# An attention and MLP block whose rounded keys and queries are stored once and repeated by the loads, with another order of work at the start and the fourth pair's load moved ahead of the third's

## The chip, the core and the metric

The kernel runs on one core of one Trainium2 chip. A core has a tensor engine (PE; PEld is its weight load), a vector engine (DVE), a scalar engine (ACT), GpSimd (POOL) and a sync engine (SP), whose queue issues nearly all transfers of this kernel, and sixteen DMA engines that carry them out. The metric is the device time of one execution in microseconds; the time of a kernel is the median of its runs. The profile is one further execution.

## The reference

One transformer block on `x` of 2048 rows by 512, in fp32, with a conditioning vector `c`:

```python
mod = (_silu(c) @ w_mod).reshape(c.shape[0], 6, 1, -1)
sa, ca, ga, sb, cb, gb = (mod[:, 0], mod[:, 1], mod[:, 2], mod[:, 3], mod[:, 4], mod[:, 5])
h = _layernorm(x, axis=-1) * (1 + ca) + sa
x = x + ga * _A_ref(h, A_wqkv, A_wo)      # 32 heads of 16, full softmax, output projection
h = _layernorm(x, axis=-1) * (1 + cb) + sb
x = x + gb * _B_ref(h, B_w1, B_b1, B_w2)  # dense to 1792, x*tanh(softplus(x)), dense to 512
```

## The kernel before

**Split operands.** The tensor engine is fed numbers in a rounded format (fp32r). To keep the accuracy, an operand is split into a rounded part (`hi`) and the rounded rest (`lo`), and a product is computed as hi*hi + hi*lo + lo*hi. For the scores the three products are folded into one contraction: a head has 16 channels, and 48 rows of a 64-row half of the array hold, for each channel, the keys' hi, lo, hi against the queries' hi, hi, lo. Two more rows of the query tile hold the negated row maxima, against ones in the key tile.

**Stages.** A start computes the conditioning columns (`modc`), the layer norm, its transposition (`h_h`, `h_l`: the hi and lo parts of the normalized rows, channels on the partitions) and the first slices of keys, queries and values, block by block of 512 rows (`tr_tb`, four blocks). Keys and queries of eight heads go to DRAM scratch (`kscr`, `qscr`) in the function `put` of `qk_unit`, and come back as pair tiles by `load_k` and `load_q`: a pair is two heads, one on partitions 0 to 47 (keys) or 0 to 49 (queries), the other on 64 to 111 or 64 to 113. The keys of a pair are 48 rows of 8 KB per head, the queries 50 rows of 2 KB. Five pairs fit (`NR`, tiles `ka`, `qa`).

**The main loop.** 512 steps t, sixteen to an iteration n of two pairs (2n and 2n+1), 32 iterations: 8 groups of four heads for each of four blocks of queries. A step has eight score products (L588, exponentials on ACT, L591), eight products for the row maxima of a later iteration, 20 steps ahead (L539 with its reduction on DVE, L541; in the 20 steps before t = 0 they are taken two at a time, L553), a few products of the projections or the MLP (L139), and the product with the values (L606). The maxima of an iteration's first pair begin at t = 16n - 20, those of its second at t = 16n - 12.

**What sets the order.** The schedule is written out by hand. `at(h, f)` runs `f` at half step h (two to a step): the position in each engine's program, not a time. The queue of SP takes its entries in order, and an entry that must wait for a buffer or for data holds all behind it. Pair 2n+1 is put in the queue at half step 32(n - 1), pair 2n at 32(n - 2) plus 2, 9 or 15; before t = 0, pairs 0 and 1 are loaded block by block within the start, and pairs 2 and 3 at the half steps of a small table (`for pp, h in ((2, -22), (3, -8))`). Row sums (`sm`), reciprocals (`rc`, `rscr`), broadcasts (`rb`, from a DRAM row read sixteen times) and the negated maxima (`mt`) take the same queue, and so do weights (`w`, `hl`, `ep`, `wm`, `wr`), values (`vq`, `vscr`, `vg`).

**PSUM.** Products go through a ring of six banks. `free_banks` takes out dependencies between instructions that only share the ring's tensor, if they touch other banks and no common tile.

Of the kernel before, what the change touches and what calls it, by code (L numbers as in the profile page):

```python
# [8 lines left out]
F32 = mybir.dt.float32  # L9
# [9 lines left out]
def adaln_block(ctx: ExitStack, tc: tile.TileContext, x, wqkv, wo, w1, b1, w2, c, w_mod, out):  # L19
# [21 lines left out]
    LOV = ((1,), (), (1, 3), (1, 3))  # L41
# [10 lines left out]
    nc.scalar.preload_act_table_set("natural_log_exp_and_others")  # L52
# [4 lines left out]
    kscr = dram.tile([H, 48, S], F32, name="kscr")  # L57
    qscr = dram.tile([H, 50, S], F32, name="qscr")
# [16 lines left out]
    sel = cst.tile([P, 1], F32, name="sel")  # L75
    nc.gpsimd.memset(sel, 0.0)
    for k in range(DK):
        nc.gpsimd.memset(sel[32 * k:32 * k + 1, :], 1.0)
# [89 lines left out]
    def free_banks():  # L168


        seen = []
        for i in nc.cur_bb.bb.instructions:
            banks, names, made = set(), set(), set()
            for a in (*i.outs, *i.ins):
                v = getattr(a, "bass_ap", None)
                if v is not None and v.tensor.name != ring_t.tensor.name:
                    names.add(v.tensor.name)
                    if any(a is w for w in i.outs):
                        made.add(v.tensor.name)
# [66 lines left out]
    def qk_unit(kind, ct, tb, tag):  # L246
# [7 lines left out]
        def fin(h=None):  # L254
            qh = qp.tile([P, TB], F32R, tag="qh", name="qh", bufs=2)
            ql = qp.tile([P, TB], F32R, tag="ql", name="ql", bufs=2)
            if h is None:
                hi_copy("a", qh, acc)
                lo_sub("v", ql, acc, qh)
            else:  # L260
                qf = pw.tile([P, TB], F32, tag="raw", name="qf", bufs=1)
                nc.scalar.copy(qf, acc)  # L262
                hi_copy("p", qh, qf)
                lo_sub("p", ql, qf, qh)
            scr, rows = (qscr, 50) if kind == 0 else (kscr, 48)
# [12 lines left out]

            put() if h is None else at(clear(h + (5 if h > 60 else 2)), put)
# [26 lines left out]
    def load_q(pp, rows=50):  # L306
# [5 lines left out]
        for s in range(2):  # L312
            nc.sync.dma_start(qt[64 * s:64 * s + rows, :], qscr[h + s, :rows, qb * TB:(qb + 1) * TB])

    def load_k(pp, tb=None):
# [3 lines left out]
        at_ = slice(0, S) if tb is None else slice(tb * TB, (tb + 1) * TB)  # L319
        assert {(1, h // 8, i) for i in (range(NB) if tb is None else (tb,))} <= put_away, (pp, put_away)  # L320
        for s in range(2):
            nc.sync.dma_start(kt[64 * s:64 * s + 48, at_], kscr[h + s, :, at_])
# [6 lines left out]
    with ExitStack() as es:  # L329
        lp = es.enter_context(tc.tile_pool(name="lp", bufs=1))  # L330
        cc = lp.tile([P, DK], F32, name="cc")
        nc.sync.dma_start(cc, c.rearrange("o (k p) -> p (o k)", p=P))
# [7 lines left out]
        wma = [lp.tile([P, DK, D], F32, name=f"wma{i}") for i in range(2)]  # L340
# [13 lines left out]
        nc.gpsimd.memset(zer, 0.0)  # L354
        for i in range(NR):
            nc.gpsimd.memset(qa[i].bitcast(F32), 0.0)
        for i in range(2):
            nc.gpsimd.memset(ka[i].bitcast(F32), 1.0)

        e = lp.tile([P, DK], F32, name="sil_e")  # L360
# [3 lines left out]
        nc.vector.tensor_mul(sil, cc, e)  # L364

# [21 lines left out]
        def first_norm():  # L387

            mv = lp.tile([P, 4, 2], F32, tag="ln_mv4", name="ln_mv4", bufs=2)
            rs = lp.tile([P, 4, 4], F32, tag="ln_rs4", name="ln_rs4", bufs=3)  # L390
            for h in range(2):
                two = slice(2 * h, 2 * h + 2)
                for i in range(2 * h, 2 * h + 2):
                    st_ = lp.tile([P, 6], F32, tag="ln_st", name="ln_st", bufs=4)
                    nc.vector.bn_stats(out=st_, in_=xts[i])
                    nc.vector.bn_aggr(out=mv[:, i, :], in_=st_)
                nc.gpsimd.tensor_scalar(rs[:, 0, two], mv[:, two, 1], 1.0, EPS, op0=ALU.mult, op1=ALU.add)
                nc.gpsimd.tensor_scalar(rs[:, 3, two], mv[:, two, 0], -1.0, 0.0, op0=ALU.mult, op1=ALU.add)
                nc.gpsimd.tensor_tensor(rs[:, 1, two], rs[:, 0, two], nhalf.to_broadcast([P, 2]), op=ALU.pow)
                nc.gpsimd.tensor_mul(rs[:, 2, two], rs[:, 3, two], rs[:, 1, two])  # L400
                if h == 0:
                    hi_k = split_hi(1, 0)
            return rs, hi_k

        def split_hi(kind, i, eng="p"):
# [4 lines left out]
        def split_lo(kind, i, hi):  # L410
            lo = lp.tile([P, DK, P], F32R, tag="wl", name="wl", bufs=2)
            lo_sub("p", lo, slices[kind, i], hi)
            slices[kind, i] = (hi, lo)

        def first_apply(rs, i, eng):
            xt = xts[i]
            if eng == "a":
                nc.scalar.activation(xt, xt, AF.Identity, scale=rs[:, 1, i:i + 1], bias=rs[:, 2, i:i + 1])
            else:
                nc.vector.tensor_scalar(xt, xt, rs[:, 1, i:i + 1], rs[:, 2, i:i + 1], op0=ALU.mult, op1=ALU.add)  # L420

        def first_tr():
            pts = [bank(("ring", "ms", "ring", "acc")[k]) for k in range(DK)]
            for ii in ((0,), (1,), (2, 3)):
                for k in range(DK):
                    for i in ii:
                        nc.tensor.transpose(pts[k][:, i * P:(i + 1) * P], xts[i][:, k * P:(k + 1) * P], ident)
            return pts

        def tr_tb(tb, ks=range(DK), pts=None):  # L430
            for k in ks:
# [12 lines left out]
        rs, hi_k = first_norm()  # L444
        pr, pm = [], bank()[:, :2 * DK].rearrange("p (i k) -> p i k", k=DK)
        for i in range(2):
            pr.append(ring())
            for k in range(DK):
                nc.tensor.matmul(pr[i][32 * k:32 * k + 32, :], sil[:, k:k + 1].to_broadcast([P, 32]), wma[i][:, k, :],
                                 start=True, stop=True)  # L450
        for i in range(2):
            row = lp.tile([P, D], F32, tag="hf", name="row", bufs=6)
            nc.scalar.copy(row, pr[i])
            for k in range(DK):
                nc.tensor.matmul(pm[:, i, k:k + 1], row[:, k * P:(k + 1) * P], sel, start=True, stop=True)
        for i in range(2):
            first_apply(rs, i, "a")
        split_lo(1, 0, hi_k)
        hi_q = split_hi(0, 0, "a")
        split_lo(0, 0, hi_q)  # L460
        first_apply(rs, 2, "a")
        first_apply(rs, 3, "v")
        nc.vector.tensor_scalar_add(modc[:, 1, :], pm[:, 1, :], 1.0)
        nc.vector.tensor_copy(modc[:, 0, :], pm[:, 0, :])
        stats_tb(1)
        tr_tb(0, pts=first_tr())
        apply_tb(1)
        def constants():
            for q4 in range(S // TB):
                nc.sync.dma_start(dap(qscr, 48 * S + q4 * TB, [[50 * S, H], [S, 2], [1, TB]]), zer[:64, :])  # L470
# [8 lines left out]
        for tb in range(NB):  # L479
            if tb + 2 < NB:  # L480
                stats_tb(tb + 2)
            if tb == 0:
                slice_split(2, 0, eng="v")
# [1024 lines left out]
    for pp, h in ((2, -22), (3, -8)):  # L1508
# [41 lines left out]
```

## Time and profile before

| | us |
|---|---|
| median of 3 runs (lowest, highest) | 1691.56 (1690.99, 1694.38) |
| profiled execution | 1691.02 |
| its span | 1689.2 |
| tensor engine busy | 1667.3 |
| vector, scalar, GpSimd busy | 1441.5, 1355.1, 821.1 |
| first write of `h_h` | 19.07 |
| first product of the maxima (L553) | 50.34 |
| first score of the main loop (L588) | 101.88 |

A busy time counts an instruction from its start to its modelled end, waits inside it included; the chain that ended last says which engine's work the end waited for. In a row of the timeline stand the start, the time, the engine, the line, the operation, output<-input, and a count where rows were merged; in a row of waits the waiting engine and line, what it waited for, and the total, the number and the longest of the waits. In the DMA view, each digit is the busy share of the sixteen engines in one fortieth of the window. A completion is written by a packet of 4 bytes, one from each DMA engine that took part in a transfer.

### The profile page before, as it was taken

Reading aid. Unit: us, or ns where it says so; the run is one execution under the profiler, and the core shown is the slowest. Engines: PE = TensorE matmul, PEld = TensorE weight load, DVE = VectorE, ACT = ScalarE, POOL = GpSimd, SP = SyncE. Lnnn points to the kernel's source line nnn. Section 1 sums busy time; section 2 is a strip of 40 time slices with the busy share of each in tenths; the row PEclk is TensorE's granted clock in tenths of the full one; section 3 lists DMA queues with packets and bytes.
Section 4 is the critical chain, followed back from the end, with each engine's and each line's share of the span. In section 5 each row is a group of like instructions: output and inputs, shape, how many; then the busy total and the mean of one; then the engine's idle time right before and its main releaser. Section 6 shows DMA issues by size and latency. Waiting matters only on the chain.

```text
span 1689.2 us, 33772 instructions
## 1 busy us (share of the span) xinstructions
PE 1667.3 (99%) x12418; PEld 921.5 (55%) x12418; DVE 1441.5 (85%) x2369; ACT 1355.1 (80%) x2612; POOL 821.1 (49%) x843
## 2 busy tenths in 40 slices
PE   7999999999999999999999999999999999999999
PEld 5755655555444455555555455555555455555687
DVE  8898888888989988888889888888889888883377
ACT  6257777777778998888888998888888998889674
POOL 7555224655313564556323564556323565555442
PEclk9999999999999999999999999999999999999999
DMA  7877556777755443434355434534354533533261
GB/s 248 269 244 199 147 150 185 218 223 216 231 142 146 110 94 98 117 88 129 84 137 152 115 77 93 139 77 127 87 144 122 130 94 77 144 107 132 75 230 63
DMA packets 115406, 238.98 MB, mean 141 GB/s; under 512 B 24928, under 2 KB 50544, under 8 KB 109288
## 3 DMA queue, kind: packets, MB, share of 16 engines
q1 hardware_dynamic: 115240, 236.82, 49.9%
q8 instruction: 98, 1.61, 0.4%
q14 instruction: 68, 0.56, 0.1%
HBM read 180.48 MB, written 51.45 MB: 137 GB/s over the span
## 4 chain that ended last, share of the span: by engine, by line
PE 91%; DVE 3%; ACT 3%; DMA 2%; POOL 1%; issue 1%; SPq 0%; ACTq 0%; DVEq 0%; POOLq 0%
PE bk L606 29%; PE ring L588 22%; PE ring L539 20%; PE bk L139 11%; PE bk L132 3%; PE ring L1219 2%; PE ring L132 2%; DVE mx L541 2%; ACT pr L591 1%; PE ring L553 0%; DMA qa<-mt 0%; DMA xt<-in_A_x 0%; PE ring L922 0%; DMA kscr<-qh 0%; PE ring L568 0%
## 5 line engine op out<-in xcount | busy, mean ns | idle before, releaser
L541 DVE TENSOR_REDUCE mx<-ring 128x1 f32<-128x512 f32 x1968 | 1223.1, 682 | 150.0 <-PE ring L539 136.4
L591 ACT ACTIVATE pr<-ring 128x512 f32<-128x512 f32 x2048 | 1078.4, 603 | 207.1 <-PE bk L139 124.7
L539 PE MATMUL ring<-ka,qa 64*128 64x512 f32 x1968 | 817.9, 429 | 1.4 <-ACT pr L591 1.1
L588 PE MATMUL ring<-qa,ka 64*128 64x512 f32 x2048 | 759.1, 402 | 3.4 <-ACT pr L591 1.9
L606 PE MATMUL bk<-pr,vg 128*32 128x512 f32 x4096 | 545.1, 604 | 0.0
L539 PEld LDWEIGHTS ring<-ka,qa 64*128 64x128 f32 x1968 | 350.5, 184 | 326.2 <-DVE mx L541 251.3
L588 PEld LDWEIGHTS ring<-qa,ka 64*128 64x128 f32 x2048 | 373.7, 184 | 194.7 <-DVE mx L541 111.4
L139 PE MATMUL bk<-h,w 64*128 64x512 f32 (+1 forms) x1080 | 278.1, 390 | 0.0
L139 PE MATMUL bk<-w,a_h 64*128 64x512 f32 x632 | 210.9, 413 | 0.0
L139 PEld LDWEIGHTS bk<-h,w 64*128 64x128 f32 x1080 | 178.5, 184 | 9.3 <-ACT pr L591 1.5
L606 PEld LDWEIGHTS bk<-pr,vg 128*32 128x32 f32 x4096 | 81.2, 108 | 135.4 <-issue 126.0
L139 PE MATMUL bk<-w,a_l 64*128 64x512 f32 x316 | 124.0, 392 | 0.0
L139 PEld LDWEIGHTS bk<-w,a_h 64*128 64x128 f32 x632 | 106.8, 184 | 4.3 <-ACT hb L800 1.0
L978 POOL TENSOR_TENSOR y<-yd,y 128x512 f32<-128x512 f32 x44 | 56.9, 1293 | 89.0 <-ACT yd L977 79.7
L812 POOL TENSOR_SCALAR qq<-ee 128x512 f32<-128x512 f32 x25 | 15.5, 619 | 169.6 <-ACT ee L806 169.6
L828 POOL TENSOR_TENSOR qq<-qq,rr 128x512 f32<-128x512 f32 x42 | 54.1, 1289 | 85.9 <-ACT rr L822 85.9
L814 POOL TENSOR_TENSOR hb<-hb,ee 128x512 f32<-128x512 f32 x42 | 54.1, 1288 | 79.6 <-DVE ee L810 77.7
L139 PE MATMUL bk<-w,o_hl 64*128 64x512 f32 x288 | 79.1, 405 | 0.0
L101 POOL TENSOR_TENSOR a_l<-hb,a_h 128x512 fp32r<-128x512 f32 x53 | 73.1, 1379 | 4.4
L98 POOL TENSOR_SCALAR qh<-qf 128x512 fp32r<-128x512 f32 x27 | 16.7, 619 | 90.8 <-ACT qf L262 69.4
L139 PEld LDWEIGHTS bk<-w,a_l 64*128 64x128 f32 x316 | 58.3, 185 | 3.4
L139 PE MATMUL bk<-h_h,wl 64*128 64x512 f32 x168 | 57.2, 420 | 0.2 <-ACT pr L591 0.2
(219 smaller groups left out, 1909.1 us busy)
## 6 DMA issues: line engine op xcount, KB each, us to landing
ka<-kscr SPq DMA_DIRECT2D x124, 384.0 KB
w<-w2scr SPq DMA_DIRECT2D x56, 512.0 KB
w<-w1scr SPq DMA_DIRECT2D x46, 512.0 KB
vg<-vscr SPq DMA_DIRECT2D x32, 552.0 KB
qa<-qscr SPq DMA_DIRECT2D x124, 100.0 KB
kscr<-qh SPq DMA_DIRECT2D x16, 512.0 KB
qscr<-qh SPq DMA_DIRECT2D x32, 256.0 KB
w2scr<-hl SPq DMA_DIRECT2D x14, 512.0 KB
```

What stands on the lines that cost most here:

```text
L101: (nc.gpsimd if eng == "p" else nc.vector).tensor_sub(lo, src, hi.bitcast(F32))
L132: nc.tensor.matmul(acc, l, r, start=start, stop=stop)
L139: i = nc.tensor.matmul(acc, l[64 * g:64 * g + 64], r[64 * g:64 * g + 64], start=start and not then, stop=bool(stop and then))
L539: nc.tensor.matmul(pm, qt[64 * s:64 * s + 64, qs * P:(qs + 1) * P], kt[64 * s:64 * s + 64, kb * TB:(kb + 1) * TB], start=True, stop=True)
L541: nc.vector.tensor_reduce(out=mxs[n][:, s, 4 * j + qs, kb:kb + 1], in_=pm, op=ALU.max, axis=AX.X)
L588: nc.tensor.matmul(p_, kt[64 * s:64 * s + 64, kc * P:(kc + 1) * P], qt[64 * s:64 * s + 64, :], start=True, stop=True)
L591: e = nc.scalar.activation(pr, p_, AF.Exp, scale=SCALE)
L606: nc.tensor.matmul(accs[n][32 * h:32 * h + 32, :], vgs[n][:, o:o + 32], pts.pop((t, h)), start=(kc == 0), stop=(kc == 15))
L814: (nc.vector if tail else nc.gpsimd).tensor_mul(hb, hb, ee)
L828: nc.gpsimd.tensor_mul(qq, qq, rr)
L978: nc.gpsimd.tensor_add(y[i], yd, y[i])
L1219: nc.tensor.matmul(po[i // 2][:, i % 2, :], l[:, s], w[:, r, :], start=(f == 0 and j == 0), stop=(f == FT - 1 and j == 2))
```

## The change

**Scratch and loads.** `kscr` shrinks from 48 to 32 rows a head and `qscr` from 50 to 34: hi once, then lo (then two rows of zeros for the queries). `put` stores hi and lo once each, for keys and queries alike, as 8 heads x 16 rows x 512. `load_q` and `load_k` now take two transfers a head in place of one: one reads the 16 hi rows twice, by a leading dimension of count 2 and step 0, into 32 partitions, the other reads the lo rows (with the two zero rows, 18 for the queries) once. A pair takes eight transfers in place of four; the rows in the tile stand in blocks of 16 (keys lo, hi, hi; queries hi, hi, lo) in place of interleaved by channel.

**Order before t = 0.** Pair 3's load moves from half step -8 to -32, ahead of pair 2's at -22.

**Start.** The x tiles are loaded first; `w_mod`'s two slices come as four tiles each; `c` is loaded as four rows by ACT's queue and transposed on PE. PE runs 38 transpositions of the identity whose result nothing reads (`keep_busy`). The conditioning sums contract on PE (`mod_sums`, accumulated over four tiles, then one transposition). The layer norm's statistics go in twos. The vector engine's `hf` is now scale times input minus `h_h` in one pass, and the shift is added by DVE or POOL. The ones in the first two key tiles are written by ACT, two query tiles' zeros move later on POOL. In `free_banks`, parts of `h_h` count as tiles of their own.

```diff
-    kscr = dram.tile([H, 48, S], F32, name="kscr")
-    qscr = dram.tile([H, 50, S], F32, name="qscr")
+    kscr = dram.tile([H, 32, S], F32, name="kscr")
+    qscr = dram.tile([H, 34, S], F32, name="qscr")
...
-                if kind == 0:
-                    for r, src in enumerate((qh, qh, ql)):
-                        nc.sync.dma_start(dap(scr, o + r * S, [[rows * S, 8], [3 * S, DH], [1, TB]]), src.bitcast(F32))
-                    return
-                hi = qh.bitcast(F32)
-                twice = bass.AP(tensor=hi.tensor, offset=hi.offset, ap=[list(hi.ap)[0], [0, 2], [1, TB]])
-                nc.sync.dma_start(dap(scr, o, [[3 * S, P], [2 * S, 2], [1, TB]]), twice)
-                nc.sync.dma_start(dap(scr, o + S, [[3 * S, P], [1, TB]]), ql.bitcast(F32))
+                for r, src in enumerate((qh, ql)):
+                    nc.sync.dma_start(dap(scr, o + r * DH * S, [[rows * S, 8], [S, DH], [1, TB]]), src.bitcast(F32))
...
-            nc.sync.dma_start(qt[64 * s:64 * s + rows, :], qscr[h + s, :rows, qb * TB:(qb + 1) * TB])
+            b, o = 64 * s, (h + s) * 34 * S + qb * TB
+            nc.sync.dma_start(qt[b:b + 32, :], dap(qscr, o, [[0, 2], [S, DH], [1, TB]]))
+            nc.sync.dma_start(qt[b + 32:b + rows, :], dap(qscr, o + DH * S, [[S, rows - 32], [1, TB]]))
...
-            nc.sync.dma_start(kt[64 * s:64 * s + 48, at_], kscr[h + s, :, at_])
+            b, o = 64 * s, (h + s) * 32 * S + at_.start
+            nc.sync.dma_start(kt[b:b + DH, at_], dap(kscr, o + DH * S, [[S, DH], [1, w]]))
+            nc.sync.dma_start(kt[b + DH:b + 48, at_], dap(kscr, o, [[0, 2], [S, DH], [1, w]]))
...
-        for i in range(2):
-            nc.sync.dma_start(wma[i], w_mod[:, i * D:(i + 1) * D].rearrange("(k p) m -> p k m", p=P))
...
         for t in range(4):
             load_x(t)
+        load_mod(0)
         slice_load(1, 0, lp, lp)
+        load_mod(1)
         slice_load(0, 0, lp, lp)
...
+        keep_busy(8)
+        cc = ring()[:, :DK]
+        nc.tensor.transpose(cc, crow, ident[:DK, :DK])
+        keep_busy(26)
...
-                nc.vector.tensor_scalar(hf, pt, modc[:, 1, k:k + 1], modc[:, 0, k:k + 1], op0=ALU.mult, op1=ALU.add)
-                lo_sub("v" if k in LOV[tb] else "p", h_l[:, k, s], hf, h_h[:, k, s])
+                nc.vector.scalar_tensor_tensor(hf, pt, modc[:, 1, k:k + 1], h_h[:, k, s].bitcast(F32), op0=ALU.mult,
+                                               op1=ALU.subtract)
+                if k in LOV[tb]:
+                    nc.vector.tensor_scalar_add(h_l[:, k, s], hf, modc[:, 0, k:k + 1])
+                else:
+                    nc.gpsimd.tensor_add(h_l[:, k, s], hf, modc[:, 0, k:k + 1].to_broadcast([P, TB]))
...
-    for pp, h in ((2, -22), (3, -8)):
+    for pp, h in ((2, -22), (3, -32)):
         at(h, lambda pp=pp: load_pair(pp))
```

The queue of SP at the end of the start, before (`ka_630` and `qa_109` are the third pair's tiles):

```order
L234 DMA wr<-in_A_wqkv 128x4x128
L1458 DMA ep<-in_B_w 128x4x128 x3
L298 DMA vscr<-vq 128x4x272
L1458 DMA ep<-in_B_w 128x4x128
L1466 DMA w1scr<-ep 128x512 x2
L1458 DMA ep<-in_B_w 128x4x128
L298 DMA vscr<-vq 128x4x272
L1466 DMA w1scr<-ep 128x512 x2
L1458 DMA ep<-in_B_w 128x4x128
L313 DMA qa_109<-qscr 50x512 x2
L322 DMA ka_630<-kscr 48x2048 x2
```

The same place now (`ka_720` and `qa_103` are the fourth pair's tiles; the sizes are those of the destination):

```order
L230 DMA wr<-in_A_wqkv 128x4x128
L1486 DMA ep<-in_B_w 128x4x128 x2
L304 DMA qa_103<-qscr 32x1x512
L305 DMA qa_103<-qscr 18x512
L304 DMA qa_103<-qscr 32x1x512
L305 DMA qa_103<-qscr 18x512
L315 DMA ka_720<-kscr 16x2048
L316 DMA ka_720<-kscr 32x1x2048
L315 DMA ka_720<-kscr 16x2048
L316 DMA ka_720<-kscr 32x1x2048
```

The fourth pair's load, eight transfers, now stands behind two of the six `ep` loads; the third pair's eight follow after four more `ep` loads, two `vscr` and four `w1scr` stores.

The queue of SP within the start, one block's stores of keys and the loads of the first two pairs' keys from it, before:

```order
L276 DMA kscr<-qh 128x2x512
L277 DMA kscr<-ql 128x512
L322 DMA ka_105<-kscr 48x512 x2
L322 DMA ka_106<-kscr 48x512 x2
L298 DMA vscr<-vq 128x4x272
```

And now:

```order
L267 DMA kscr<-qh 8x16x512
L267 DMA kscr<-ql 8x16x512
L315 DMA ka_98<-kscr 16x512
L316 DMA ka_98<-kscr 32x1x512
L315 DMA ka_98<-kscr 16x512
L316 DMA ka_98<-kscr 32x1x512
L315 DMA ka_99<-kscr 16x512
L316 DMA ka_99<-kscr 32x1x512
L315 DMA ka_99<-kscr 16x512
L316 DMA ka_99<-kscr 32x1x512
```

The two stores are 256 KB each (before 512 and 256 KB), and four loads have become eight; outside the start the pair loads keep their places among the other transfers.

More of the change, by code (lines that the diff above doesn't have):

```diff
@@ L264, in fin @@
                 lo_sub("p", ql, qf, qh)
-            scr, rows = (qscr, 50) if kind == 0 else (kscr, 48)
+            scr, rows = (qscr, 34) if kind == 0 else (kscr, 32)
             def put():
@@ L353, in adaln_block, with keep_busy @@
         zer = lp.tile([P, TB], F32, name="zer")
[L354 to L358, printed above, removed]
+        for t in qa[:3]:
+            nc.gpsimd.memset(t.bitcast(F32), 0.0)
+        spare = ring()
+        def keep_busy(n):
+            for _ in range(n):
+                nc.tensor.transpose(spare[:, :P], ident, ident)
+        keep_busy(8)
+        cc = ring()[:, :DK]
+        nc.tensor.transpose(cc, crow, ident[:DK, :DK])
+        keep_busy(26)
         e = lp.tile([P, DK], F32, name="sil_e")
@@ L364, in adaln_block @@
         nc.vector.tensor_mul(sil, cc, e)
+        hi_copy("a", ka[0], ones.to_broadcast([P, S]))
         rss = {}
@@ L451, in adaln_block @@
[L451 to L462, printed above, removed]
@@ new lines, in adaln_block @@
+        for q in range(2):
+            stats_two(q)
+        first_apply(3, "p")
+        for t in (*(t.bitcast(F32) for t in qa[3:]), zer):
+            nc.gpsimd.memset(t, 0.0)
+        mod_sums(0, (0, 1))
+        first_apply(0)
+        first_tr(0)
+        mod_sums(0, (2,))
+        first_apply(1)
+        first_tr(1)
+        mod_sums(0, (3,))
+        first_apply(2)
+        first_tr(2)
+        first_tr(3)
+        mod_cols(0)
+        hi_k = split_hi(1, 0, "a")
+        hi_copy("a", ka[1], ones.to_broadcast([P, S]))
```

121 lines of the change are left out of this document (64 added, 57 removed).

## The prediction

> **What bounds the kernel now.** I read the page first (busy shares, the chain that ended last), then the waits of the tensor engine, then the DMA view in short windows, then the timeline of the sync queue around one load.
>
> ```profile
> span 1689.2 us, 33772 instructions
> PE 1667.3 (99%) x12418; PEld 921.5 (55%) x12418; DVE 1441.5 (85%) x2369; ACT 1355.1 (80%) x2612; POOL 821.1 (49%) x843
> PE 91%; DVE 3%; ACT 3%; DMA 2%; POOL 1%; issue 1%; SPq 0%; ACTq 0%; DVEq 0%; POOLq 0%
> q1 hardware_dynamic: 115240, 236.82, 49.9%
> ```
>
> The tensor engine carries 91% of the chain. The DMA engines are busy half the time on average, with 2% of the chain: the loads are hidden. How narrowly is the question.
>
> ```profile
> PE ring L449 <- DVE sil L364: 9.2, 1, 9.2
> PE ring L588 <- DMA qa<-mt: 1.2, 1, 1.2
> ```
>
> In the waits of the tensor engine itself, one is for the start (9.2 us) and one, of 1.2 us, is for a transfer. So everything outside the first 20 us is won or lost in whether a load still comes in time.
>
> **How many engines a transfer uses.** Three windows of the DMA view, each with one kind of transfer in flight:
>
> ```profile
> DMA packets 69, 0.15 MB, mean 104 GB/s; under 512 B 4, under 2 KB 4, under 8 KB 68
> q1 hardware_dynamic: 68, 0.13, 24.7%
> DMA packets 365, 0.70 MB, mean 176 GB/s; under 512 B 22, under 2 KB 22, under 8 KB 365
> q1 hardware_dynamic: 365, 0.70, 49.3%
> DMA  0000990939990341929229197994909103000000
> DMA packets 144, 0.52 MB, mean 194 GB/s; under 512 B 16, under 2 KB 16, under 8 KB 144
> ```
>
> First pair (543.70 to 545.12 us): `rb<-rscr`, 64 rows of 2 KB, whose DRAM side is written as 4 x 16 with the 16 a repeat of step 0. It is 64 data packets and 4 completion packets, at a quarter of the sixteen engines: it runs on four. Second pair (33 to 37 us): three `qscr` stores in a row, DRAM side 8 x 16 x 512, at half of the sixteen for four microseconds: eight engines, and the same eight, since three transfers waiting on different eights would have filled sixteen. Third (976.3 to 979 us): one `w<-w1scr`, 128 rows, 16 completion packets: sixteen engines. So the number of engines follows the outermost count of the narrower side: 4, 8, 16. Per engine that is 104/4 = 26 GB/s and 176/8 = 22 GB/s; I take 25, and for a bad case 194 GB/s over the third window's 16 engines at 63.5% busy, 19.
>
> The change writes the repeated halves of its loads as `[[0,2],[S,16],[1,w]]`: outermost count 2, on 32 partitions. By the rows that is two engines, always the same two. No row has a bulk transfer with an outermost 2, so the bounds are 2 and 16 engines; I take 2, since `rb` is the same form with another count. The Trainium skill, "DMA: Bandwidth & Descriptors", section "Why a DMA increments its semaphore by 16 and not by 1", states it: the number is the largest up to 16 that divides both sides' slowest dimension, and on this path the lowest-numbered engines are taken; its "Rules for kernel authors" warn of a leading zero-stride broadcast of c copies, which leaves at most c. The trace agrees at 4, 8 and 16; at 2 no run here shows it yet.
>
> **The loads in the main loop.** The work of a pair of heads on engines 0 and 1 becomes: keys 2 x 256 KB on two engines, 2 x 131072 B / 25 GB/s = 10.5 us; queries 2 x 64 KB, 2.6 us; the 16-row and 18-row parts 1.0 us (8 KB and 4 KB per engine and half). Together 14.1 us, where the 968 KB over sixteen engines took some 4. Now the time there is, for pair 31:
>
> ```profile
> 751.26 0.67 SPq L313 DMA_DIRECT2D qa<-qscr  x2
> 751.98 0.78 SPq L322 DMA_DIRECT2D ka<-kscr  x2
> 751.41 1.06 PE L606 MATMUL bk<-pr,vg 128*32 128x512 f32 x8
> 754.24 1.06 PE L606 MATMUL bk<-pr,vg 128*32 128x512 f32 x8
> 757.13 1.06 PE L606 MATMUL bk<-pr,vg 128*32 128x512 f32 x8
> 760.16 1.07 PE L606 MATMUL bk<-pr,vg 128*32 128x512 f32 x8
> 762.99 1.06 PE L606 MATMUL bk<-pr,vg 128*32 128x512 f32 x8
> SPq L313 <- PE ring L539: 97.3, 32, 4.4
> 975.63 0.32 SPq L751 DMA_DIRECT2D w<-w1scr  x1
> ```
>
> Each L606 row closes one step of 2.87 us. An odd pair 2n+1 is loaded when iteration n-1 begins, and the issue itself waits for the tensor engine to leave the buffer (32 waits of L313, 97.3 us), so it can't go sooner. Its first products stand four steps later, after the row of 762.99, at 764.05. From issue to first packet is 0.95 us (the `w` issue of 975.63; the window above begins at 976.3 with four empty slices of 0.0675 us). The last key row lands at 751.26 + 0.95 + 14.1 = 766.3: 2.3 us late, and both halves of the tile are used at once, so nothing starts earlier. I add 0.5 us for what stands ahead in the two queues (a 512 KB transfer is 1.3 us per engine, ahead in some four of ten cases). There are 30 odd pairs from 5 to 63: 30 x 2.8 = 84 us.
>
> Even pairs mostly have 15 to 30 us and arrive in time. Five (4, 12, 16, 18, 52) are issued 10 to 14 us ahead; pair 16:
>
> ```profile
> 401.78 3.07 SPq L313 DMA_DIRECT2D qa<-qscr  x2
> 413.86 1.07 PE L606 MATMUL bk<-pr,vg 128*32 128x512 f32 x8
> 146.52 0.67 SPq L313 DMA_DIRECT2D qa<-qscr  x2
> 149.43 1.38 SPq L313 DMA_DIRECT2D qa<-qscr  x2
> 160.96 0.60 SPq L631 DMA_DIRECT2D sm<-ot  x1
> 168.19 0.24 DVE L641 RECIPROCAL rc<-sm 128x16 f32<-128x16 f32 x1
> ```
>
> 401.78 + 15.05 = 416.8 against 414.9, 2 us without a queue ahead and 8 with half a pair; 5 each, 25 us. Four times (pairs 6, 8, 10, 14) an even pair follows its odd one within 3 us, and the small `sm` load stands behind both: 146.52 + 0.95 + 28.2 = 175.7, where the vector engine wants it at 168.19 plus the 2.3 us by which that iteration has slipped. 5 us late; less the 1.4 us of products that the six ring banks still take (a step's 2.87 us without its 1.06 us is eight products, 0.23 each), 3.5 each, 14 us. A stall counts in full only where the chain is on the tensor engine, 91%: (84 + 25 + 14) x 0.91 = 112 us. The four more issues per pair (0.39 us each, row 751.98) end ahead of the transfers and cost nothing while two engines are the limit.
>
> **The prologue.**
>
> ```profile
> 60.00:110.00 50.00, 49.26 (x282) 33.04 (x280) 46.40 (x48) 14.43 (x30) 27.22 (x28) 1.00 0.96 304
> 37.62 1.74 SPq L313 DMA_DIRECT2D qa<-qscr  x4
> 91.31 0.73 PE L553 MATMUL ring<-ka,qa 64*128 64x512 f32 x4
> 94.67 2.98 SPq L577 DMA_DIRECT2D qa<-mt  x4
> 101.88 0.49 PE L588 MATMUL ring<-qa,ka 64*128 64x512 f32 x1
> ```
>
> From 60 to 110 us the DMA engines are already 96% busy. Two engines now get more: from the first query loads (37.62 before, some 33 now) to the end of the third pair's load stand 5.2 us of queries, 4 x 5.6 of block loads, 3 x 2.6 of key stores (now 8 x 16, eight engines, two stores of 256 KB in place of 768 KB), 14.1 for the fourth pair, moved ahead of the third in the sync queue, 14.1 for the third, and 7.3 of weight and value transfers: 71 us, so the third pair lands at about 104. Its first product stands at 91.31 before, and at 84 if the start gains what is worked out below. The wait eats that gain and 12 us more. The row sums (`qa<-mt`) then stand behind some 12 us of stores, with 10.6 us of work (91.31 to 101.88) to hide them: 2 to 3 more. First score at 117 in place of 101.9: +15 us, from +5 (if the stores keep up) to +30. The fourth pair's earlier place alone frees the queue at 88 us, but it was never waited for.
>
> **The start.**
>
> ```profile
> 0.00:10.00 10.00, 0.79 (x4) 0.20 (x8) 6.17 (x6) 1.49 (x2) 7.88 (x26) 1.00 0.78 274
> 10.00:20.00 10.00, 9.79 (x49) 7.09 (x41) 7.70 (x20) 4.74 (x8) 5.73 (x11) 1.00 1.07 393
> 2.31 7.47 DMA xt<-in_A_x
> 19.07 0.78 ACT L440 ACTIVATE h_h<-ring,modc 128x512 fp32r<-128x512 f32 x1 [2.93 <-PE ring L427]
> 17.11 0.42 PE L427 MATMUL ring<-ident,xt 128*128 128x128 f32 x1
> 34.00 0.60 PE L435 MATMUL ring<-ident,xt 128*128 128x128 f32 x4
> ```
>
> The four x tiles come 2 MB of `w_mod` sooner (landing 9.78 before, about 5 now). What gates the first `h_h` is then the second half of `w_mod`, behind 3.25 MB: 8 to 11 us at 393 to 274 GB/s plus 2, then row copy, transposition and add, about 1.5: `h_h` at 13 in place of 19.07, -6, and about -1 from the vector engine's shorter second pass (a scalar add for a subtraction on some tiles). -7, between -3 and -9; it is inside the +15 above, since the third pair's wait takes it up.
>
> The warm-up transposes are priced at nothing: the engine had nothing to do there. A transposition took 0.22 us at 17.11 and 0.11 us in the group of 34.00, though the granted clock reads 1.00 throughout. The Trainium skill, "TensorE: Matmul & The Clock Gate", Part 4, says that transposes don't count as activity; by it the warm-up fails, the start gains 2 us less, and the sum would be 2 us more. No run here shows it yet.
>
> **The sum.** +15 + 112 = +127 us on the profiled execution's own 1691.0 us (span 1689.2): 1818. The median of the runs shown, 1691.56, is 0.5 above it, nothing beside these terms. Within 0.2% (3.4 us) a measurement can't tell a change.
>
> **The rivals.**
> - Not narrowed, the other sign: the loads spread over sixteen engines, or successive ones take different engines. Decided by the first repeated key load. Then only the start is left, 1691.0 - 7 = 1684. For it: no row has a leading repeat. Against: `rb`, and the stores that stayed on the same eight. 0.06, nearly all of it faster.
> - Narrowed but covered: the odd pair in time, only prologue and a few even pairs late, 1691.0 + 15 to 45 = 1706 to 1736. It needs 764.05 - 751.26 - 0.95 = 11.8 us for a pair, or 30 GB/s per engine; no window shows that. 0.10.
> - Narrowed, with slower packets: at 19 GB/s a pair takes 18.6 us, 6.8 late; 30 x 7.3 + 50 + 36 = 305, times 0.91 = 278, prologue +30: 1999. For it: two engines read the same rows. Against: `rb` does too, at 26. 0.12 (1890 to 2030).
> - The forecast, two engines at 24 to 26 GB/s, 1760 to 1890: 0.72.
>
> The range 1715 to 1930 leaves out the first and the outer parts of the second and third, 0.18. Faster 0.06, same 0.01, slower 0.93.
>
> **What would show it.** Right: in a window with only a pair's load in flight, the DMA share at an eighth and two completion packets for each repeated load; waits of the tensor engine for `ka<-kscr` of 2 to 3 us, about once per iteration; a wait of some 15 us for it near 90 us; `h_h` first at about 13 us; steps between these waits at 2.87 us as before. Wrong: no such waits and a share near one during the loads (first rival), or waits of 7 us and more per iteration (third).

## The result, and the profile after

The changed kernel takes 2051.3 us (median; 2043.6 to 2060.6) against 1691.8 us, 1.2127 times as long, 95% interval 1.2106 to 1.2147. The forecast was 1818 us, between 1715 and 1930: the sign is right, the size is not. The profiled execution of the changed kernel has a span of 2045.0 us, 355.8 more than before's 1689.2; the working below is made on these two.

The page of the changed kernel, its head, the row of the granted clock, the DMA queue and the chain that ended last by engine:

```profile
span 2045.0 us, 34291 instructions
PEclk9878889888988999999898989999999999999999
q1 hardware_dynamic: 110740, 228.43, 35.9%
PE 56%; DMA 32%; SPq 5%; DVE 2%; ACT 2%; issue 2%; POOL 1%; POOLq 0%; ACTq 0%; DVEq 0%
```

The DMA engines are on average less busy than before (35.9% for 49.9%), and yet a third of the chain is now theirs (2% before). The row of the granted clock, all full before, has dips. The waits of the tensor engine say which transfers:

```profile
PE ring L567 <- DMA ka<-kscr: 146.7, 34, 6.6
PE ring L567 <- DMA od<-ot: 23.9, 5, 5.7
PE bk L127 <- POOL wl L96: 21.0, 1, 21.0
PE ring L581 <- DMA ka<-kscr: 4.8, 1, 4.8
```

Before, the one wait for a transfer in this list was 1.2 us. Now 34 products of the loop wait for keys, 146.7 us in all. The five waits put down to `od<-ot` stand at the same place of five more odd pairs (37, 41, 43, 47, 51), before a product that reads only `ka` and `qa`. In the prologue, a single wait of 21.0 us is for the weights of the values, and one of 4.8 us for the third pair's keys.

To see where the 355.8 us lie, the span is cut at the end of the first group of output products (L606 before, L634 after) and at the end of the last: prologue, main loop, tail. The rows are the end of the prologue and the loop; each gives the stretch, its length, the busy time and count of each engine, the granted clock, the DMA share and GB/s. Before, and then after:

```profile
60.00:110.30 50.30, 49.56 (x284) 33.30 (x284) 46.40 (x48) 14.43 (x30) 27.52 (x28) 1.00 0.97 304
110.30:1588.40 1478.10, 1472.27 (x11414) 771.55 (x11411) 1269.92 (x2142) 1253.57 (x2448) 718.57 (x714) 1.00 0.49 131
```

```profile
60.00:153.20 93.20, 59.11 (x295) 38.49 (x296) 48.33 (x50) 14.78 (x31) 26.25 (x27) 0.80 0.50 158
153.20:1944.00 1790.80, 1568.25 (x11414) 817.54 (x11413) 1278.86 (x2142) 1264.39 (x2448) 718.21 (x714) 0.92 0.35 106
```

The prologue is 42.9 us longer (153.2 for 110.3; forecast +15), the main loop 312.7 (1790.8 for 1478.1; forecast +112), the tail, what is left of the spans, 0.2 at most. In the loop the tensor engine runs the same 11414 products. They are busy for 96.0 us more (1568.25 for 1472.27, at a mean clock of 0.92), and the engine stands idle for 216.7 us more (222.55 for 5.83). So nearly a third of the loop's loss is not waiting but slow work, which the forecast did not have at all. (A step holds four score products and four for the maxima, 2048 and 1968 over 512 steps, not eight of each as the description of the kernel before has it.)

One odd pair, 59, step by step. The sync queue, then the tensor engine, then two windows of the DMA view (the first with 40 slices of 0.1 us from 1736.7, the second from 1743 to 1745):

```profile
1736.71 0.63 SPq L304 DMA_DIRECT2D qa<-qscr  x1
1739.38 0.60 SPq L316 DMA_DIRECT2D ka<-kscr  x1
```

```profile
1748.36 1.06 PE L634 MATMUL bk<-pr,vg 128*32 128x512 f32 x8
1754.27 0.76 PE L567 MATMUL ring<-ka,qa 64*128 64x512 f32 x1 [4.85 <-DMA ka<-kscr]
1757.55 1.93 PE L634 MATMUL bk<-pr,vg 128*32 128x512 f32 x8
```

```profile
DMA  0000000000000011133333711111132029993019
...
DMA packets 15, 0.11 MB, mean 53 GB/s; under 512 B 2, under 2 KB 2, under 8 KB 2
q1 hardware_dynamic: 15, 0.11, 13.4%
```

From 1743 to 1745 nothing but the repeated key load is in flight: 53 GB/s at 13.4% of sixteen engines, which is two engines at 26 GB/s each. The narrowing is as forecast, and so is the need: the pair is wanted 1749.4 - 1736.7 = 12.7 us after its first issue. But the products start 17.6 us after it, where the forecast had 15.05 and half a microsecond for a queue. The first packets come 1.4 us after the issue (fourteen empty slices; 0.95 assumed). By the packets' records the repeated keys' 8 KB packets, 0.31 us each, run from 1742.7 to 1753.5: the queries and the short parts ahead of them took 4.6 us (3.6 assumed), the keys themselves 10.8 (10.5 assumed), and 0.8 us more pass before the product starts. After the wait the eight output products take 1.93 us where they took 1.06 before it.

Over the 28 odd pairs that wait as this one does (17 and 21 wait a step later), the same reading gives a mean of 12.8 us from first issue to need (forecast 12.8) and 18.5 us from first issue to products (forecast 15.55); with a `w` load between, pairs took up to 2.5 us longer than pair 59. The steps with these waits, read as the time from one group of output products to the next, are 7.7 us too long in the mean, 5.3 of it idle and 2.4 at the slower clock.

### The profile page after: what moved, and what is told of

Read it like the earlier page. It is cut to its first block, busy times and chain, and to the rows that moved or that the text cites. A ratio compares the mean times of both kernels' runs of the same rounds, so it can differ in the third digit from the quotient of the medians.

```text
span 2045.0 us, 34291 instructions
## 1 busy us (share of the span) xinstructions
PE 1775.2 (87%) x12491; PEld 974.6 (48%) x12491; DVE 1442.7 (71%) x2372; ACT 1368.8 (67%) x2612; POOL 810.8 (40%) x839
## 3 DMA queue, kind: packets, MB, share of 16 engines
q1 hardware_dynamic: 110740, 228.43, 35.9%
## 4 chain that ended last, share of the span: by engine, by line
PE 56%; DMA 32%; SPq 5%; DVE 2%; ACT 2%; issue 2%; POOL 1%; POOLq 0%; ACTq 0%; DVEq 0%
DMA ka<-kscr 19%; PE bk L634 16%; PE ring L616 13%; PE ring L567 12%; PE bk L134 6%; DMA sm<-ot 3%; DMA qa<-qscr 2%; PE bk L127 2%; PE ring L127 2%; PE ring L1247 2%; DMA od<-ot 2%; SPq L304 2%; SPq L305 1%; DVE mx L569 1%; ACT pr L619 1%
## 5 line engine op out<-in xcount | busy, mean ns | idle before, releaser
L619 ACT ACTIVATE pr<-ring 128x512 f32<-128x512 f32 x2048 | 1089.5, 603 | 495.2 <-PE bk L134 335.5
L567 PE MATMUL ring<-ka,qa 64*128 64x512 f32 x1968 | 858.3, 448 | 185.7 <-DMA ka<-kscr 146.7
L616 PE MATMUL ring<-qa,ka 64*128 64x512 f32 x2048 | 792.1, 419 | 36.7 <-DVE mx L569 28.9
L567 PEld LDWEIGHTS ring<-ka,qa 64*128 64x128 f32 x1968 | 371.8, 194 | 536.8 <-DVE mx L569 232.0
L634 PE MATMUL bk<-pr,vg 128*32 128x512 f32 x4096 | 572.7, 633 | 0.0
L616 PEld LDWEIGHTS ring<-qa,ka 64*128 64x128 f32 x2048 | 394.3, 194 | 233.7 <-DVE mx L569 143.7
L134 PE MATMUL bk<-h,w 64*128 64x512 f32 (+1 forms) x1080 | 287.6, 401 | 0.6 <-DMA w<-w1scr 0.6
L134 PE MATMUL bk<-w,a_h 64*128 64x512 f32 x632 | 223.1, 434 | 0.0
L634 PEld LDWEIGHTS bk<-pr,vg 128*32 128x32 f32 x4096 | 83.0, 110 | 148.2 <-issue 138.9
L583 DVE TENSOR_REDUCE mx<-ring 128x2 f32<-128x1024 f32 x40 | 46.9, 1219 | 39.4 <-PE ring L581 38.9
```

The lines of the kernel that those rows point to most:

```text
L134: i = nc.tensor.matmul(acc, l[64 * g:64 * g + 64], r[64 * g:64 * g + 64], start=start and not then, stop=bool(stop and then))
L567: nc.tensor.matmul(pm, qt[64 * s:64 * s + 64, qs * P:(qs + 1) * P], kt[64 * s:64 * s + 64, kb * TB:(kb + 1) * TB], start=True, stop=True)
L583: nc.vector.tensor_reduce(out=mxs[n][:, :, jq, kb:kb + 1], in_=pm, op=ALU.max, axis=AX.X)
L616: nc.tensor.matmul(p_, kt[64 * s:64 * s + 64, kc * P:(kc + 1) * P], qt[64 * s:64 * s + 64, :], start=True, stop=True)
L619: e = nc.scalar.activation(pr, p_, AF.Exp, scale=SCALE)
L634: nc.tensor.matmul(accs[n][32 * h:32 * h + 32, :], vgs[n][:, o:o + 32], pts.pop((t, h)), start=(kc == 0), stop=(kc == 15))
```

## The experiments

All times are set against runs of the kernel before on the same chip.

### All repeated loads on sixteen engines

```diff
-            nc.sync.dma_start(qt[b:b + 32, :], dap(qscr, o, [[0, 2], [S, DH], [1, TB]]))
+            for r in range(2):
+                nc.sync.dma_start(qt[b + 16 * r:b + 16 * r + 16, :], dap(qscr, o, [[S, DH], [1, TB]]))
...
-            nc.sync.dma_start(kt[b + DH:b + 48, at_], dap(kscr, o, [[0, 2], [S, DH], [1, w]]))
+            for r in (DH, 2 * DH):
+                nc.sync.dma_start(kt[b + r:b + r + DH, at_], dap(kscr, o, [[S, DH], [1, w]]))
```

> The changed kernel with every repeated load written as two loads of 16 rows in place of one of 2 x 16 rows; stores, order and start as changed. Theory (the two-engine loads carry the whole loss): the loop's steps are back at 2.87 us, only the start's gain is left (h_h at 14.4 in place of 19.1): 1682 to 1692 us, no wait for ka<-kscr above 1 us, clock 1.00. Rival (storing once and reading the same rows twice, or the new load order, costs by itself): it stays above 1750 us.

Measured: 1723.9 us, ratio 1.0197 (1.0180 to 1.0214). Of the 360 us, 327 go with the outer count of 2. The row of its windows for the loop, 136.1 to 1621.6:

```profile
136.10:1621.60 1485.50, 1476.20 (x11414) 775.34 (x11413) 1269.64 (x2142) 1254.15 (x2448) 720.41 (x714) 1.00 0.52 127
```

The loop is back at 1485.5 us, the clock at 1.00. But the theory missed the prologue: first output products at 136.1 for 110.3, and the wait for the weights of the values is still there, at 11.4 us. So something else in the change costs some 26 us there.

### Which loads: keys or queries

Each time one of the two edits above alone.

> The changed kernel with only the repeated key loads written as two loads of 16 rows; the queries' stay on two engines. Theory (lateness is bytes per engine): a pair needs about 2.6 us for its queries on two engines and 2 to 3 for the rest, well inside 13 us: 1682 to 1700 us. Rival (any two-engine load holds up what is queued behind it, on all engines): 1750 us and more.

> The changed kernel with only the repeated query loads written as two loads of 16 rows; the keys' stay on two engines. Theory (an odd pair is 5.3 us late as measured, and a half-speed stretch of about 2.3 us follows a wait): the pair gains 2.6 us, so it is 2.5 to 3 us late, 29 x (2.7 + 1 to 2.3) = 105 to 145, prologue +35, even pairs and small loads +40: 1870 to 1910 us. Rival (the forecast's sizes, 2.8 us late with no half-speed stretch): the odd pairs are in time, about 1740 us.

Measured: keys on sixteen engines, queries on two: 1758.7 us, 1.0414 (1.0378 to 1.0450). Queries on sixteen, keys on two: 2003.4 us, 1.1850 (1.1829 to 1.1870). Both theories missed; the first result lies at its rival's 1750 us and more. The queries alone on two engines still cost 35 us over the kernel with sixteen for all, 28 of them in the loop, where small loads stand behind them. And freeing the queries' 2.6 us for the keys brought much less than 2.6 us per odd pair: the loop went from 1790.8 to 1744.3 us only. Part of the reason is in the rows of the sync queue above. The first repeated key load isn't issued until 2.7 us after the first query load, so most of the queries' time on two engines passes while the keys are still being issued. In one pair of this run (first issued at 1697.18) the repeated keys' packets begin 4.2 us after the first issue, where it was 6.0 in pair 59: 1.8 us sooner, not 2.6, and the products start 16.6 us after it. A pair's time is not simply the sum of its bytes over two engines, as the forecast's 14.1 us was.

### The same start and order, with the scratch of before

`kscr` and `qscr` with 48 and 50 rows, and the stores and loads of before.

> The changed kernel with the scratch, stores and loads of before (48 and 50 rows stored, one load of them); new start and the fourth pair sooner stay. Theory: 1682 to 1692 us, as the kernel with 16-row loads, since neither the start nor the order costs anything. Rival (the fourth pair's earlier place blocks the preparations of the weights by itself): 1700 us and more.

Measured: 1694.0 us, 1.0014 (1.0005 to 1.0024). The stores and loads of the rounded rows carry all of the loss but some 2.5 us, and the gain that the theory counted on isn't there. Taken apart further:

> The kernel with the scratch, stores and loads of before and the new start, with the fourth pair's load back behind the third's: the new start alone. Theory (the 4.7 us that h_h comes sooner are used up by the sync queue: 3.3 us at the first key store, 0.8 at the first query load, none at the third block of keys): 1689 to 1693 us, the same as before. Rival (the gain carries through, and only the fourth pair's place hid it): 1685 to 1688 us.

> The kernel before with nothing but the fourth pair's load moved ahead (-32 in place of -8). Theory (it fills the engines between 64 and 80 us, where the weights' transfers wait behind it, and the values' weights come late): 1693 to 1696 us. Rival (the place doesn't matter): 1690.5 to 1692 us.

Measured: the new start alone 1692.0 us, 0.9999 (0.9990 to 1.0009); the fourth pair sooner alone 1694.0 us, 1.0013 (1.0004 to 1.0022). Both theories hold. The start's gain is made and lost. Both kernels' rows in time, before and with the new start and the order:

```profile
19.07 0.78 ACT L440 ACTIVATE h_h<-ring,modc 128x512 fp32r<-128x512 f32 x1 [2.93 <-PE ring L427]
27.94 0.37 SPq L276 DMA_DIRECT2D kscr<-qh  x1
37.62 1.74 SPq L313 DMA_DIRECT2D qa<-qscr  x4
52.68 1.94 SPq L322 DMA_DIRECT2D ka<-kscr  x4
```

```profile
12.57 7.31 SPq L334 DMA_DIRECT2D xt<-in_A_x  x8
20.98 2.55 SPq L502 DMA_DIRECT2D qscr<-zer  x4
24.99 2.15 SPq L272 DMA_DIRECT2D kscr<-qh  x1
36.80 1.82 SPq L309 DMA_DIRECT2D qa<-qscr  x4
52.71 1.72 SPq L318 DMA_DIRECT2D ka<-kscr  x4
```

The first `h_h` comes 4.7 us sooner (14.4 in the changed kernel), the first key store 3, the first query load 0.8, the third block of key loads not at all. Until 25 us the sync queue still issues loads and constants (the eight `xt` issues alone take 7.3 us), and the first store stands behind them.

### Keys stored on sixteen engines

What is left with 16-row loads? The stores of the keys were written with an outer count of 128 before, and are written 8 x 16 now. This kernel is the one with 16-row loads, and the hi and lo rows alternate in `kscr`:

```diff
+                    if kind == 1:
+                        nc.sync.dma_start(dap(scr, o + r * S, [[2 * S, P], [1, TB]]), src.bitcast(F32))
+                        continue
                     nc.sync.dma_start(dap(scr, o + r * DH * S, [[rows * S, 8], [S, DH], [1, TB]]), src.bitcast(F32))
```

> As the kernel with 16-row loads, and the keys stored with the two halves' rows alternating, so that the store's outer count is 128 in place of 8 (sixteen engines, as before the change). Theory (what is left there, +32 us, is the stores of the keys: 512 KB on eight engines take 5 us where 768 KB on sixteen took 2.5, and the next loads wait for them on the sync queue): the waits of 11.4 and 3.5 us for the weights near 85 to 100 us go, first output product at 112 to 118 in place of 136: 1692 to 1703 us. Rival (24 issues per block of keys on the sync queue in place of 8 are the cause): 1715 to 1725 us.

Measured: 1714.5 us, 1.0135 (1.0119 to 1.0151): 9.4 us better, less than the theory's 21 to 32, and just below the rival's range. The wait for the weights of the values, which the theory had go, stayed (12.9 us; the shorter one fell from 3.5 to 0.7). (The expectation counts issues wrongly: the rows of the sync queue show 12 per block of keys in place of 4, not 24 in place of 8.) Both causes act. In the prologue each block of keys is stored, its loads wait on the sync queue until it has landed, and the next block's store stands behind these loads. The rows of that queue, before, with 16-row loads, and with the stores on sixteen engines as well:

```profile
55.22 0.38 SPq L277 DMA_DIRECT2D kscr<-ql  x1
58.59 1.99 SPq L322 DMA_DIRECT2D ka<-kscr  x4
60.63 0.45 SPq L234 DMA_DIRECT2D wr<-in_A_wqkv  x1
```

```profile
58.29 0.87 SPq L267 DMA_DIRECT2D kscr<-ql  x1
65.50 0.31 SPq L316 DMA_DIRECT2D ka<-kscr  x1
...
82.78 0.42 SPq L230 DMA_DIRECT2D wr<-in_A_wqkv  x1
```

```profile
55.94 0.94 SPq L268 DMA_DIRECT2D kscr<-ql  x1
61.24 0.32 SPq L319 DMA_DIRECT2D ka<-kscr  x1
...
75.72 0.42 SPq L230 DMA_DIRECT2D wr<-in_A_wqkv  x1
```

From the end of the store's issue to the first load's it takes 3.0 us before, 6.3 with the stores on eight engines, 4.4 with sixteen; issuing a block's loads takes 2 us before and 5.6 with 12 issues. So the weights of the values (`wr`), which stand behind all blocks, are issued at 60.6, 82.8 and 75.7 us, and in the changed kernel at 80.2.

### Stored once, with the repeat inside

Can the rows be stored once without these costs? Keys alternate and are stored as above; the repeat of the queries is written inside the 16 rows, and the keys are loaded as all 32 alternating rows and then the 16 hi rows again:

```diff
-            nc.sync.dma_start(qt[b:b + 32, :], dap(qscr, o, [[0, 2], [S, DH], [1, TB]]))
+            nc.sync.dma_start(qt[b:b + 32, :], dap(qscr, o, [[S, DH], [0, 2], [1, TB]]))
...
-            nc.sync.dma_start(kt[b:b + DH, at_], dap(kscr, o + DH * S, [[S, DH], [1, w]]))
-            nc.sync.dma_start(kt[b + DH:b + 48, at_], dap(kscr, o, [[0, 2], [S, DH], [1, w]]))
+            nc.sync.dma_start(kt[b:b + 32, at_], dap(kscr, o, [[S, 32], [1, w]]))
+            nc.sync.dma_start(kt[b + 32:b + 48, at_], dap(kscr, o, [[2 * S, DH], [1, w]]))
```

> Rounded values stored once, keys' rows alternating and stored on sixteen engines; the repeat of the queries written inside the 16 rows (outer count 16, one load), keys as one load of 32 rows and one of 16. Theory (the outer count alone decides): no wait for a load above 1 us, 8 issues per pair as in the changed kernel: 1688 to 1700 us. Rival (a repeated read is slow in itself): waits for qa<-qscr or ka<-kscr, 1710 us and more.

> Rounded values stored once with the repeat inside, and the fourth pair's load behind the third's. Theory (that place costs some 2.5 us): 1695 to 1697 us; rival (it doesn't matter here): 1698 to 1701 us.

Measured: 1698.9 us, 1.0041 (1.0026 to 1.0055), and with the fourth pair behind the third 1697.8 us, 1.0031 (1.0019 to 1.0044). The theory holds for the loop; the row of its windows for the first of the two:

```profile
117.70:1597.60 1479.90, 1474.40 (x11414) 773.78 (x11413) 1269.27 (x2142) 1253.67 (x2448) 720.08 (x714) 1.00 0.48 127
```

With as many issues as the changed kernel and the same bytes stored, only the shape of the access patterns differs, and 352 us are gone. It still doesn't beat the kernel before: fewer bytes bring nothing where transfers are hidden, and the prologue is 7 us longer (117.7 for 110.3). Twice the issues per block (8 for 4) is the likely cause of a part of that, but no run changes them alone. For the second kernel the intervals can't tell the two expectations apart. No experiment points to a version faster than before.

### The fourth pair back behind the third, loads on two engines

> The changed kernel with the fourth pair's load back in its place behind the third's; loads stay on two engines. Theory (the weights near 85 to 110 us queue behind that pair's two-engine load): the wait of 21 us for them falls by 8 to 14, 2035 to 2043 us. Rival (the place of that load doesn't matter, since the other loads fill the two engines as well): 2048 to 2054 us.

Measured: 2056.0 us, 1.2157 (1.2139 to 1.2174): no gain, and near the rival's 2048 to 2054; the 5 us above the changed kernel lie within that kernel's own runs (2043.6 to 2060.6). In the waits of its tensor engine, the one for the weights did fall, from 21.0 to 6.3 us, but another took its place:

```profile
PE ring L616 <- DMA qa<-mt: 23.6, 2, 17.5
PE bk L127 <- POOL wl L96: 6.3, 1, 6.3
```

What now comes late are the negated maxima (`qa<-mt`) and not the weights. While two engines are full, the order of what goes over them chose only who waits.

### The tensor engine kept at work while it waits

```diff
             pm = ring()
+            if (j, s, qs, kb) == (1, 1, 0, 0) and n > 1:
+                ko, qo = ka[2 * n % NR], qa[2 * n % NR]
+                for f in range(22):
+                    nc.tensor.matmul(pm, qo[64:128, :P], ko[64:128, :TB], start=True, stop=True)
```

> The changed kernel with 22 idle products (about 5 us) ahead of the first product of each odd pair from 5 on, so that the tensor engine is at work while it waits; their results are overwritten by the product itself. Theory (a wait of 4 to 6.6 us drops the clock to half, which costs about 2.3 us behind each of 28 waits): 64 us less, 5 to 15 back where the filling is longer than the wait: 1990 to 2005 us, granted clock 0.95 or more. Rival (the slow products have another cause, as the traffic of the loads): 2045 to 2065 us.

Measured: 2029.3 us, 1.1997 (1.1980 to 1.2014), between the two. The mechanism is as the theory has it, and the granted clock came out at 0.96. The tensor engine's rows in time for pair 59 again, with the 22 idle products, and the products after them at 0.39 and 1.06 us:

```profile
1736.80 5.26 PE L570 MATMUL ring<-ka,qa 64*128 64x512 f32 x22
1742.07 0.46 PE L571 MATMUL ring<-ka,qa 64*128 64x512 f32 x1
1742.38 0.39 PE L620 MATMUL ring<-qa,ka 64*128 64x512 f32 x1
1743.93 1.06 PE L638 MATMUL bk<-pr,vg 128*32 128x512 f32 x8
```

The loop's row of this kernel's windows:

```profile
156.00:1927.20 1771.20, 1668.12 (x12074) 918.84 (x12071) 1273.90 (x2142) 1260.83 (x2448) 719.34 (x714) 0.96 0.35 107
```

The 660 idle products are busy for 164 us, and by the trace's records 15 of these run beside real ones, so the real ones are busy for 1519 us in place of 1568.3: 49 of the 96 us of slow work are gone. The time without a real product is 1771 - 1519 = 252 us where 222.6 were idle, 30 more. The net is 20 in the loop. Part of the 30 is filling that outlasted the wait it replaced, part may be longer waits at the next late transfers; the run does not divide them.

### Odd pairs on sixteen engines, even pairs on two

> The changed kernel with 16-row loads for the first four pairs and for the odd pairs after them; the even pairs from 4 on stay on two engines. Theory (losses add up by place): the odd pairs' 222 us go, of the 47 behind small loads that stand behind two pair loads half or more, of the prologue's 43 some 17 (to the level of the kernel with 16-row loads); the five even pairs' 36 stay: 1750 to 1800 us. Rival (the two engines are full, so that the waits move to the even pairs): 1850 us and more.

Measured: 1827.4 us, 1.0798 (1.0784 to 1.0813), between the two. Against the changed kernel 223.9 us are gone: 14.6 of the span in the prologue and 205.9 in the loop. Against the kernel with 16-row loads 103 are left, 99 in the loop (1584.9 for 1485.5 us). The steps of that loop, read as the time from one group of output products to the next, put some 56 us at the even pairs (48 at the first step of eight of them, 8 at the step after), 5 at one wait for the negated maxima, and 36 at the four places where a small load stands behind an even pair's; the theory had these 36 fall, and they did not.

## Why the prediction was right, and where it was wrong

**Two engines for an outer count of 2: right.** 53 GB/s and 13.4% of sixteen engines are two engines. The Trainium skill, "DMA: Bandwidth & Descriptors", section "Rules for kernel authors", has it that a leading zero-stride broadcast of c copies is confined to at most c engines; the trace now agrees at 2, as it did at 4, 8 and 16. At 26 GB/s per engine the third rival's slower packets are excluded, although its time (1999 us, 1890 to 2030) came nearest to the result: it had nearly the right total for a reason that was not there.

**The odd pairs, 30 x 2.8 = 84, times 0.91: the step that failed.** It came to 206 us in the loop by the run with the odd pairs on sixteen engines. The window for a pair was right (12.8 us). Two sizes and one term were wrong. The pair took 18.5 us and not 15.55: in pair 59 the first packets came 0.45 us later than assumed, the queries and short parts took 1.0 us longer, the keys 0.3, and 0.8 us from the last packet to the product had been left out; pairs with a `w` load between took longer still. Where the load is late anyway, three more microseconds of transfer are all wait: 5.3 us in place of 2.8. And the forecast let the tensor engine resume at full speed. After a wait it ran at half the clock for some 3 to 6 us, 2.4 us lost per wait in the mean. The clock of before read 1.00 throughout, so no row of it had this price, but the Trainium skill did: "TensorE: Matmul & The Clock Gate", section "HAM oscillation — how this bites in real kernels", warns of gaps above some 3.4 us, and the forecast, which cited another part of that page, did not use it. The trace agrees for the waits of 4.4 us and more. It was no separate cost that could be added, though: the run with the filled waits took away 49 of the 96 us of slow work, and the loop gained 20.

**Even pairs 25 and small loads 14: mis-sized.** Together 99 us (times as run) for 36. By the steps of the run with the odd pairs on sixteen engines, eight even pairs came late (4, 12, 16, 20, 28, 32, 36, 52), where the forecast had five (4, 12, 16, 18, 52). The small loads were furthest off, 36 us for 14 and not gone with the odd pairs. `sm`, issued at 227.49, is used 39.7 us after the first issue of the two pair loads ahead of it (200.88), where the forecast counted 29.2, and the vector engine waits for it for 10.0 us and not 5, as its row in time shows:

```profile
240.55 0.25 DVE L669 RECIPROCAL rc<-sm 128x16 f32<-128x16 f32 x1 [10.03 <-DMA sm<-ot]
```

The forecast added up transfers and took the sync queue to be free meanwhile. It was not. Of two like issues ahead of that `sm`, the odd pair's took 0.43 us and the even pair's held the queue for 8.92:

```profile
201.56 0.43 SPq L305 DMA_DIRECT2D qa<-qscr  x1
208.35 8.92 SPq L305 DMA_DIRECT2D qa<-qscr  x1
```

What held that issue the profile doesn't name. Besides, the transfers of this queue report to eight semaphores in turn in the trace, and an issue stands until the transfer eight places ahead of it has landed. A pair's load is now eight transfers, and was four. One row of the queue's waits, where before the largest row for key loads came to 9.0 us:

```profile
SPq L304 <- DMA ka<-kscr: 42.7, 13, 5.4
```

No run separates what either cost in the changed kernel.

**The prologue, +15: the mechanism was another.** The third pair was late, as forecast, but by 4.8 us. The forecast counted 71 us of transfers on two engines and asked when the last lands. What set the pace was the sync queue: store, wait, loads, store, for each block of keys. The stores on eight engines were seen and counted as time on those engines, not as a wait of the queue. That four more issues per pair cost nothing held for the loop where loads are on sixteen engines (1479.9 us for 1478.1), and not for a block of the prologue. Behind this stood the values' weights, which the forecast didn't follow. From the kernels' first output products, taken in the order of these steps, the 42.9 us divide into some 17 for the loads on two engines (153.2 to 136.1), 7 for the stores on eight (to 129.4), 12 for the third load per head of keys and queries (to 117.7), 2 for the fourth pair's place (to 115.4) and 5 for the rest.

**The start, -7: made and not kept.** 4.7 us at `h_h`, nothing 35 us later.

**The warm-up transposes at nothing: not tested.** No run leaves them out. That transposes raise the clock is shown below, so the 2 us that the prediction would have added by the page's rule had no ground here.

## What to carry to other kernels

Put the count that divides by sixteen outermost on the DRAM side of every transfer, stores too: the same bytes cost 350 us more written with outer counts of 2 and 8 than with 16 and 128. Where a transfer has a margin of a few microseconds, forecast the wait with all that is small (first packet, last packet, the short parts ahead of the bulk), and add the half-speed stretch that followed each wait of some 4 us and more of the tensor engine here. A queue that stores, waits and loads in turn is a chain of its own: count its issues and the landing of what it stored or loaded before, not only the bytes.

## What the runs showed of the hardware

A group of eight output products took 1.06 us ahead of a wait and 1.93 behind it in most waits of 4.4 us and more, and shorter waits can do the same; from the changed kernel:

```profile
711.67 0.46 PE L567 MATMUL ring<-ka,qa 64*128 64x512 f32 x1 [1.93 <-DMA ka<-kscr]
712.30 1.94 PE L634 MATMUL bk<-pr,vg 128*32 128x512 f32 x8
```

Transposes alone raise the clock. In the changed kernel the tensor engine runs nothing but 34 transposes of the identity and one small one until 7.5 us. Two windows of it, and the first products of the kernel before, which has no such warm-up:

```profile
3.70 1.91 PE L361 MATMUL ring<-ident 128*128 128x128 f32 x8
5.91 1.36 PE L361 MATMUL ring<-ident 128*128 128x128 f32 x11
```

```profile
19.99 1.19 PE L132 MATMUL ring<-h_h,wh 128*128 128x512 f32 x2
23.06 0.62 PE L132 MATMUL ring<-h_h,wh 128*128 128x512 f32 x2
```

The changed kernel's transposes start 0.21 us apart until 5.6 us, and 0.11 from 5.8 us on, some 4.5 us after the first. The Trainium skill, "TensorE: Matmul & The Clock Gate", Part 4, has it that they don't count as activity; this trace differs. Before, the first products ran at half speed until about 22 us, behind 16 transposes from 16.2 us on that were also 0.21 us apart. The row of the granted clock reads 1.00 in both kernels for these microseconds, so there the durations say more than the row.
